# An mLSTM cell before a cosine-gated feed-forward on one Trainium2 core: the state's increment by head in two column halves, one transpose for y's last columns, and another order of the first weight conversions

## The chip, the cores and the metric

The kernel runs on one core of a Trainium2 chip. Its metric is the device time of one execution in microseconds (us). The profile that is read here is of one execution of the same program; its span is 553.4 us.

## The reference, cut to what matters

```python
batch, n_heads, seq, head_dim = (4, 8, 768, 40)          # B, H, S, D
for t in range(S):
    m_new  = np.maximum(f_gate[:, :, t] + m, i_gate[:, :, t])
    f_stab = np.exp(f_gate[:, :, t] + m - m_new)
    i_stab = np.exp(i_gate[:, :, t] - m_new)
    m = m_new
    C = f_stab * C + i_stab * np.einsum('bhd,bhe->bhde', vt, kt)     # state, 40 x 40 for each head
    n = f_stab * n + i_stab * kt
    h_tilde = np.einsum('bhde,bhe->bhd', C, qt)
    denom   = np.maximum(np.abs(np.einsum('bhd,bhd->bh', n, qt)), 1.0)
    y[:, :, t] = sigmoid(o_gate[:, :, t]) * h_tilde / denom
x = y.transpose(0, 2, 1, 3).reshape(3072, 320)
h = x @ w_in                                             # 320 x 2048, float64
out = ((h * np.cos(h)) @ w_out).astype(float32)          # 2048 x 320, float64
```

## The kernel before, in words

The recurrence over 768 steps is computed in chunks of 128 steps. A cell is one chunk of one batch: 6 chunks by 4 batches make 24 cells, numbered n = 4 c + b. A cell computes, for its 8 heads, the scores inside the chunk (`scores`, `ps`), weighs them with the decay (`weigh`), applies them to v (`values`, `ph`), adds what the kept state gives (`values_kept`, `pq`), divides and gates (`normalize`), and makes the increment of the state for the next chunk. Cells 0 to 7 write y with time on the partitions (`z`) and turn it on TensorE (`px`); cells 8 to 23 compute y already turned (`values_turned`, `hp`) and have no `px`. The last chunk, cells 20 to 23, needs no increment.

The state's increment is `pu` = (k weighed)ᵀ · [v, 1]. `weigh_k` (L387) multiplies k, which lies in tiles of 64 elements a head with zeros behind the 40, by a weight of each step on GpSimd, 128x512 elements. `seam` (L580) then takes the heads in pairs: 104 columns of two heads' k are the stationary operand (head one at 0 to 39, head two at 64 to 103), the 82 columns of both heads' v move. Of the four blocks that come out two are wanted, those of a head with itself; they lie at partitions 0 to 39 and 64 to 103. `state` copies them (chunk 0, ScalarE, L594) or adds them (later chunks, VectorE, L596) into the kept state.

The feed-forward works on a chunk of all 4 batches, 512 tokens. `Up(c, f2)` multiplies two blocks of 128 features: the first 256 rows of x by L613, 128 rows a time, the last 64 rows by L616, where two blocks of features share the array by row halves; x's last 64 rows therefore lie twice, at partitions 0 to 63 and 64 to 127. `near` and `sin` (ScalarE), `rest` and `gate` (VectorE) make h cos h, and `down` (L645) accumulates the output. Each cell of chunk c + 1 is interleaved by hand with two `Up` and two `down` of chunk c (`both_parts`), and the order in which Python issues the work is each engine's queue order (`manual_schedule`).

`normalize` writes z in two parts: L537 writes the first 256 columns; L542 the last 64, once in chunk 0, and twice side by side in chunk 1. In chunk 1 one transpose (L571) turns these doubled 128 columns. In chunk 0 two matmuls against the identity (L575) turn the one copy of 64 columns into each half of the partitions.

The weights come as float64 bit patterns. `parts` (two ScalarE passes, L140 and L142) and `join` (three VectorE passes L146, L148, L150, and an integer addition on GpSimd, L151) make float32 of them, a piece at a time. The first `Up` needs the three pieces of w_in's first quarter: two of 512 columns (`w_in_sb`) and one of 256 (`w_in_l`, the operand of L616). The temporaries `wt` and `wm` have two buffers each.

`first_cells` (L659 to L769) orders cells 0 to 3, which nothing of the feed-forward can overlap. Its end is what the change touches:

```python
        weigh(3)
        join(*parts(*pieces.pop(0)))      # w_in, first piece
        ...
        seam_out(2); state(2); gates_keep(*pg)
        values(3); normalize(3)
        turn(B)
        join(*parts(*pieces.pop(0)))      # second piece
        warm(3); seam(3)
        decay_exponents(B); load_E(B + 2)
        seam_out(3)
        join(*parts(*pieces.pop(0)))      # third piece, w_in_l
        state(3)
```

Of the kernel before, what the change touches and what calls it, by code (L numbers as in the profile page):

```python
# [11 lines left out]
FP = mybir.dt.float32  # L12
I32 = mybir.dt.int32
# [3 lines left out]
OP = mybir.AluOpType  # L17
# [12 lines left out]
def kernel(  # L30
# [20 lines left out]
    nc = tc.nc  # L51

    B, H, S, D = q.shape
# [13 lines left out]
    DA, DL, T4 = 32, 8, 4  # L67
    assert DM - NK * 128 == 64 and NF % 4 == 0 and DA + DL == D
    NB = 4
    PR = 64 + D  # L70
    TURNED = 2 * B
    SPREAD = (0, 1)

# [68 lines left out]
        nc.scalar.activation(out=m, in_=lo, func=AF.Copy, scale=2.0 ** -29)  # L142
        return dst, hi, t, m

    def join(dst, hi, t, m):
        nc.vector.tensor_scalar(out=t.bitcast(FP), in0=t.bitcast(FP), scalar1=LEAST, scalar2=GREATEST,  # L146
                                op0=OP.max, op1=OP.min)
        nc.vector.tensor_scalar(out=t, in0=t, scalar1=5, scalar2=2, op0=OP.logical_shift_left,  # L148
                                op1=OP.logical_shift_right)
        nc.vector.scalar_tensor_tensor(out=t, in0=hi, scalar=TOP2, in1=t, op0=OP.bitwise_and, op1=OP.bitwise_or)  # L150
        nc.gpsimd.tensor_tensor(out=dst.bitcast(I32), in0=t, in1=m, op=OP.add)  # L151

    def block(f2, e):

# [203 lines left out]
    def cols(n, j, width):  # L358
        c, b = divmod(n, B)
        return tab[:, c, j, ts(b, H)].unsqueeze(2).to_broadcast([128, H, width])  # L360


    def decay_exponents(n):
        E = Es[n]
        nc.vector.tensor_tensor(out=E, in0=E, in1=cols(n, 0, C), op=OP.subtract)  # L365
        nc.gpsimd.affine_select(out=E, in_=E, compare_op=OP.is_ge, fill=1.0e30, base=0,  # L366
                                pattern=[[0, H], [1, C]], channel_multiplier=-1)
# [15 lines left out]

    def weigh_k(n):
        if n < N - B:
            kw = p2.tile([128, H, 64], FP, name="kw", tag="kw")
            nc.gpsimd.tensor_tensor(out=kw, in0=ks[n % NB], in1=cols(n, 1, 64), op=OP.mult)  # L387
            kws[n] = kw

    def psum(n):  # L390
# [3 lines left out]
    def pair(t, p):  # L394
        return t[:, 2 * p:2 * p + 2].rearrange("p j d -> p (j d)")
# [122 lines left out]
    def normalize(n):  # L518
        c, b = divmod(n, B)
        pq, hs = heads_of[n]  # L520
        if n >= B:
            ph = hs
            hs = p1.tile([128, H, D1], FP, name="hs", tag="hs")
            nc.vector.tensor_tensor(out=hs, in0=pq, in1=cols(n, 2, D1), op=OP.mult)
            nc.vector.tensor_tensor(out=hs, in0=hs, in1=ph, op=OP.add)
        dn = p2.tile([128, H], FP, name="dn", tag="dn")

        nc.vector.scalar_tensor_tensor(out=dn, in0=hs[:, :, D], scalar=-TWO_PI, in1=least, op0=OP.mult, op1=OP.max)
        nc.vector.scalar_tensor_tensor(out=dn, in0=hs[:, :, D], scalar=TWO_PI, in1=dn, op0=OP.mult, op1=OP.max)
        nc.vector.reciprocal(out=dn, in_=dn)  # L530
        y = p1.tile([128, H, D], FP, name="y", tag="y")
        o = sig[c][:, ts(b, DM)].rearrange("t (h d) -> t h d", h=H)
        nc.vector.tensor_tensor(out=y, in0=o, in1=hs[:, :, 0:D], op=OP.mult)

        z = p1.tile([128, DM + 64], FP, name="z", tag="z")
        za = z[:, 0:NK * 128].rearrange("t (i k d) -> t k i d", i=2, k=HP)
        nc.vector.tensor_tensor(out=za, in0=y[:, :, 0:DA].rearrange("t (k i) d -> t k i d", i=2),  # L537
                                in1=dn.rearrange("t (k i) -> t k i", i=2).unsqueeze(3).to_broadcast([128, HP, 2, DA]),
                                op=OP.mult)
        twice = 1 if n < B else 2  # L540
        shape = [128, twice, H, DL]
        nc.vector.tensor_tensor(out=z[:, NK * 128:NK * 128 + 64 * twice].rearrange("t (e h d) -> t e h d", e=twice, h=H),  # L542
                                in0=y[:, :, DA:D].unsqueeze(1).to_broadcast(shape),
                                in1=dn.unsqueeze(1).unsqueeze(3).to_broadcast(shape), op=OP.mult)
        ys[n] = z
# [17 lines left out]
    def seam(n):  # L563

        pool, tag = psum(n)
        if n < TURNED:
            px = pool.tile([128, NK + 1, C], FP, name="px", tag=tag)
            for i in range(NK):
                nc.tensor.transpose(px[:, i], ys[n][:, ts(i, 128)], ident)
            if n >= B:  # L570
                nc.tensor.transpose(px[:, NK], ys[n][:, NK * 128:], ident)  # L571
            else:

                for e in range(2):
                    nc.tensor.matmul(px[64 * e:64 * e + 64, NK], ys[n][:, NK * 128:DM], ident, start=True, stop=True)  # L575
            pxs[n] = px
        if n < N - B:
            pu = pool.tile([128, HP, 2, D1], FP, name="pu", tag=tag)
            for p in range(HP):
                nc.tensor.matmul(pu[0:PR, p].rearrange("p j d -> p (j d)"), pair(kws[n], p)[:, 0:PR],  # L580
                                 vs[n % NB][:, 2 * p:2 * p + 2].rearrange("p j d -> p (j d)"), start=True, stop=True)
            pus[n] = pu

    def seam_out(n):
        c, b = divmod(n, B)
        if b == 0:
            xT[c] = p2.tile([128, NK + 1, B, C], FP, name="xT", tag="xT")
        nc.scalar.copy(out=xT[c][:, :, b], in_=pxs[n])

    def state(n):  # L590
        if n < N - B:
            for j, r, s in halves(n):
                if n < B:
                    nc.scalar.copy(out=s, in_=pus[n][r, :, j])  # L594
                else:
                    nc.vector.tensor_tensor(out=s, in0=s, in1=pus[n][r, :, j], op=OP.add)  # L596


    gs, po = {}, {}
# [59 lines left out]
    def first_cells():  # L659
        nc.vector.memset(nil, 0.0)  # L660
        gates_in()
        nc.scalar.copy(out=ident_b, in_=ident)
        load(0, "qk")
        later_gates_in()
        load(0, "v")
        load(1, "qk")
        load_o(0, (0, 1))
        load(1, "v")
        load(2, "qk")
        load_E(0)  # L670
        load_E(1)
        warm(12)
        wall_in(0, 0, pmu)
        wall_in(0, 1, psum_o())
        gates_first()
        gates_first_out()
        spread(0, 0)
        decay_exponents_half(0, 0)
        turn(0)
        turn_out(0, False)  # L680
        gates_sums()
        spread(0, 1)
        decay_exponents_half(0, 1)
        decay(0)
        weigh_k(0)
        load_E(2)
        load(2, "v")
        load_E(3)
        load_o(0, (2, 3))
        load(3)  # L690
        pieces.extend(weights_in(0))
        wall_in(1, 0, psum_o())
        wall_in(1, 1, psum_o())
        gates_less_sums()
        spread(1, 0)
        decay_exponents_half(1, 0)
        scores(0)
        gates_maxima()
        turn(1)
        weigh(0)  # L700
        sigmoid(0, slice(0, 2))
        turn_out(1, False)
        spread(1, 1)
        decay_exponents_half(1, 1)
        gates_exponents()
        decay(1)
        weigh_k(1)
        values(0)
        normalize(0)
        scores(1)  # L710
        gates_exp()
        turn(2)
        turn_out(2, False)
        warm(2)
        seam(0)
        weigh(1)
        seam_out(0)
        state(0)
        load(B)
        decay_exponents(2)  # L720
        gates_diagonal()
        decay(2)
        weigh_k(2)
        values(1)
        load_E(B)
        load_o(1)
        load_E(B + 1)
        outs.append((0, weights_out(0)))
        normalize(1)
        scores(2)  # L730
        turn(3)
        sigmoid(0, slice(2, 4))
        seam(1)
        weigh(2)
        decay_exponents(3)
        turn_out(3)
        seam_out(1)
        values(2)
        decay(3)
        weigh_k(3)  # L740
        state(1)
        normalize(2)
        scores(3)
        pg = gates_turn()
        warm(1)
        seam(2)
        weigh(3)
        join(*parts(*pieces.pop(0)))
        pieces.extend(weights_in(1))
        load(B + 1)  # L750
        outs.extend((p, weights_out(p)) for p in range(1, 3))
        seam_out(2)
        state(2)
        gates_keep(*pg)
        values(3)
        normalize(3)
        turn(B)
        join(*parts(*pieces.pop(0)))
        warm(3)
        seam(3)  # L760
        decay_exponents(B)
        load_E(B + 2)
        seam_out(3)
        join(*parts(*pieces.pop(0)))
        state(3)
        turn_out(B, False)
        decay(B)
        weigh_k(B)
        sigmoid(1)  # L769
# [161 lines left out]
```

## Time and profile before

The time is 555.97 us, the median of three runs (555.28 to 556.11).

| Engine | busy us | share of the span | instructions |
|---|---|---|---|
| PE (TensorE matmul) | 542.2 | 98% | 3247 |
| PEld (weight load) | 322.9 | 58% | 3247 |
| DVE (VectorE) | 351.0 | 63% | 690 |
| ACT (ScalarE) | 262.8 | 47% | 418 |
| POOL (GpSimd) | 85.8 | 16% | 114 |

TensorE's granted clock is 1.00 in every stretch. A float32 matmul shows as two records, a float32 transpose as one. In the rows of the views, `out<-in` gives the tiles by the program's names, `128*104` the rows and columns of the stationary operand, `128x82` partitions by elements of the moving one, and `xN` how many records the row merges. In brackets stands how long the engine was idle before the row and what ended that; "issue" means that the profile shows nothing it waited for. Records of matmuls overlap[...]: the distance between starts tells what one costs in a stream.

### The profile page before, as it was taken

How to read it: one execution, taken by the hardware profiler on the slowest of the kernel's cores; microseconds unless marked ns; L12 is line 12 of the kernel's file. 1: busy time of each engine (PE TensorE's matmuls, PEld its weight loads, DVE VectorE, ACT ScalarE, POOL GpSimd, SP SyncE). 2: the span in 40 equal slices, each digit the busy share in tenths (PEclk: the TensorE clock that was granted, in tenths of full speed). 3: DMA queues.
4: the chain of work that ended last, by engine and by line, in shares of the span. 5: the costliest groups of instructions: out<-in, count | busy, mean ns of one | idle time of the engine just before them, and what ended most of it. 6: DMA issues, size and time to landing. Idle time of an engine off the chain costs nothing.

```text
span 553.4 us, 8844 instructions
## 1 busy us (share of the span) xinstructions
PE 542.2 (98%) x3247; PEld 322.9 (58%) x3247; DVE 351.0 (63%) x690; ACT 262.8 (47%) x418; POOL 85.8 (16%) x114
## 2 busy tenths in 40 slices
PE   8998999999999999999999999999999999999997
PEld 5865566665665565565555555656655655555554
DVE  5877967757777677577667667666766765322321
ACT  4869686774632544543436345327345332332312
POOL 6542533523110100101101101100000000000000
PEclk9999999999999999999999999999999999999999
DMA  9999969560265751166634065635065000000001
GB/s 141 230 199 251 237 167 226 133 149 3 72 139 119 157 118 45 49 137 141 154 82 89 13 167 129 136 79 121 7 160 120 8 15 12 30 22 1 0 0 47
DMA packets 134507, 56.80 MB, mean 103 GB/s; under 512 B 72080, under 2 KB 130528, under 8 KB 134464
## 3 DMA queue, kind: packets, MB, share of 16 engines
q1 hardware_dynamic: 134320, 56.04, 45.7%
q8 instruction: 25, 0.41, 0.3%
q0 software_dynamic: 96, 0.18, 0.1%
q14 instruction: 18, 0.15, 0.1%
q10 hardware_dynamic: 48, 0.02, 0.0%
HBM read 50.00 MB, written 6.21 MB: 102 GB/s over the span
## 4 chain that ended last, share of the span: by engine, by line
PE 90%; DVE 5%; POOL 2%; issue 1%; ACT 1%; DMA 0%; POOLq 0%; ACTq 0%; DVEq 0%
PE po L645 38%; PE pup L613 29%; PE pup L616 9%; PE ps L440 4%; PE hp L483 3%; PE pu L580 3%; PE ph L465 2%; PE hp L477 2%; DVE wt L146 1%; PE pt L421 1%; DVE wt L150 1%; DVE wt L148 1%; POOL w_out_sb L151 1%; PE pq L455 0%; DVE n L624 0%
## 5 line engine op out<-in xcount | busy, mean ns | idle before, releaser
L645 PE MATMUL po<-w_out_sb,g 128*128 128x320 f32 x768 | 218.5, 438 | 2.7 <-POOL w_out_sb L151 2.7
L645 PEld LDWEIGHTS po<-w_out_sb,g 128*128 128x128 f32 x768 | 142.1, 190 | 68.0 <-issue 8.3
L613 PE MATMUL pup<-xT,w_in_sb 128*128 128x512 f32 x384 | 175.2, 598 | 0.8 <-POOL w_in_sb L151 0.5
L621 ACT ACTIVATE n<-pup 128x512 int32<-128x512 f32 x96 | 52.0, 593 | 218.2 <-PE pup L616 218.2
L624 DVE SCALAR_TENSOR_TENSOR n<-pup,n 128x512 f32<-128x512 f32 x96 | 61.9, 686 | 139.5 <-ACT n L621 139.5
L613 PEld LDWEIGHTS pup<-xT,w_in_sb 128*128 128x128 f32 x384 | 70.8, 190 | 77.5 <-issue 66.5
L366 POOL TENSOR_SCALAR_AFFINE_SELECT E<-E 128x1024 f32<-128x1024 f32 x19 | 20.8, 1094 | 286.9 <-DVE E L365 248.3
L629 ACT ACTIVATE n<-n 128x512 f32<-128x512 f32 x96 | 58.8, 630 | 11.6 <-DVE n L624 11.6
L633 DVE SCALAR_TENSOR_TENSOR g<-pup,n 128x512 f32<-128x512 f32 x96 | 61.7, 685 | 1.7
L616 PE MATMUL pup<-xT,w_in_l 64*128 64x512 f32 x192 | 54.2, 641 | 0.9 <-POOL w_in_l L151 0.9
L616 PEld LDWEIGHTS pup<-xT,w_in_l 64*128 64x128 f32 x192 | 14.4, 184 | 37.4 <-issue 34.9
L374 ACT ACTIVATE E<-E 128x1024 f32<-128x1024 f32 x21 | 22.2, 1058 | 23.1 <-POOL E L366 18.5
L446 DVE TENSOR_TENSOR E<-ps,E 128x512 f32<-128x512 f32 x48 | 30.7, 680 | 3.4 <-PE ps L440 3.4
L405 DVE STREAM_TRANSPOSE t<-qs 128x512 f32<-128x512 f32 x32 | 32.3, 1088 | 0.0
L440 PEld LDWEIGHTS ps<-t,t 40*128 40x128 f32 (+1 forms) x384 | 25.0, 188 | 9.7 <-issue 9.2
L440 PE MATMUL ps<-t,t 40*128 40x128 f32 (+1 forms) x384 | 25.8, 274 | 0.0
L374 ACT ACT_TABLE_LOAD x18 | 23.1, 1283 | 0.3
L776 ACT ACT_TABLE_LOAD x18 | 23.1, 1283 | 0.3
L365 DVE TENSOR_TENSOR E<-E,tab 128x1024 f32<-128x1024 f32 x19 | 23.1, 1215 | 0.0
L497 DVE STREAM_TRANSPOSE room<-hp 128x128 f32<-128x128 f32 x32 | 8.6, 306 | 22.5 <-PE hp L483 22.5
L580 PEld LDWEIGHTS pu<-vs,kw 128*104 128x104 f32 x160 | 16.2, 171 | 9.8 <-issue 9.8
L387 POOL TENSOR_TENSOR kw<-ks,tab 128x512 f32<-128x512 f32 x20 | 20.9, 1043 | 0.1
(130 smaller groups left out, 444.2 us busy)
## 6 DMA issues: line engine op xcount, KB each, us to landing
E<-M_d SPq DMA_DIRECT2D x22, 512.0 KB
bits<-in_moe_w_in_dram SPq DMA_DIRECT2D x40, 128.0 KB
bits<-in_moe_w_out_dram SPq DMA_DIRECT2D x8, 640.0 KB
room<-G_d SPq DMA_DIRECT2D x32, 128.0 KB
ks<-in_k_dram SPq DMA_DIRECT2D x24, 160.0 KB
vs<-in_v_dram SPq DMA_DIRECT2D x24, 160.0 KB
out_dram<-o_sb SPq DMA_DIRECT2D x24, 160.0 KB
qs<-in_q_dram SPq DMA_DIRECT2D x32, 80.0 KB
```

Of the source, the lines that this page charges most:

```text
L374: nc.scalar.activation(out=Es[n], in_=Es[n], func=AF.Exp, scale=-1.0)
L405: nc.vector.transpose(out=dst.rearrange("r p (t x) -> r p x t", x=T4), in_=src.rearrange("r p (x d) -> r p x d", x=T4)[:, :, :, 0:32])
L440: nc.tensor.matmul(ps[j][:, p], kT[r, p], qT[r, p], start=True, stop=True)
L446: nc.vector.tensor_tensor(out=w, in0=pss[n][j], in1=w, op=OP.mult)
L580: nc.tensor.matmul(pu[0:PR, p].rearrange("p j d -> p (j d)"), pair(kws[n], p)[:, 0:PR], vs[n % NB][:, 2 * p:2 * p + 2].rearrange("p j d -> ...
L613: nc.tensor.matmul(pu, w_in_sb[:, i, ts(block(f2, e), 128)], x(i), start=(i == 0), stop=False)
L616: nc.tensor.matmul(pu, w_in_l[r, f2], x(NK, r), start=False, stop=True)
L621: nc.scalar.activation(out=self.n[e], in_=self.pu[e], func=AF.Copy, bias=0.25)
L624: nc.vector.scalar_tensor_tensor(out=self.n[e].bitcast(FP), in0=self.pu[e], scalar=0.25, in1=self.n[e], op0=OP.add, op1=OP.subtract)
L629: nc.scalar.activation(out=r, in_=r, func=AF.Sin, scale=TWO_PI_DOWN)
L633: nc.vector.scalar_tensor_tensor(out=g, in0=self.pu[e], scalar=TWO_PI, in1=self.n[e].bitcast(FP), op0=OP.mult, op1=OP.mult)
L645: nc.tensor.matmul(po[c][b], gs[c, f][:, ts(b, C)], w_out_sb[:, f], start=(f == 0), stop=(f == NF - 1))
```

## The change

Three edits. First, the increment of the state is made head by head: eight matmuls of 40 stationary and 41 moving columns in the place of four of 104 and 82. The even heads' results go to partitions 0 to 39, the odd heads' to 64 to 103 of the same PSUM tile, which is half as large, so the two heads of a pair lie in the two column halves of the array. The block products that were thrown away are not computed, `weigh_k` handles 40 elements a head and not 64, and `state` reads the same partitions as before.

Second, z's last 64 columns are written twice in chunk 0 too, and one transpose makes both halves there, as in chunk 1; the pair of matmuls against the identity is gone.

Third, in `first_cells` the second piece of w_in is joined before `gates_keep`, `values(3)` and `normalize(3)`, the third before `seam_out(3)` and cell 4's `decay_exponents`, and the third piece's integer addition is done by VectorE in the place of GpSimd. In the built program this addition is one instruction of another kind, over 128x512 16-bit halves.

```diff
-    def join(dst, hi, t, m):
+    def join(dst, hi, t, m, last=None):
...
-        nc.gpsimd.tensor_tensor(out=dst.bitcast(I32), in0=t, in1=m, op=OP.add)
+        (last or nc.gpsimd).tensor_tensor(out=dst.bitcast(I32), in0=t, in1=m, op=OP.add)
...
-            kw = p2.tile([128, H, 64], FP, name="kw", tag="kw")
-            nc.gpsimd.tensor_tensor(out=kw, in0=ks[n % NB], in1=cols(n, 1, 64), op=OP.mult)
+            kw = p2.tile([128, H, D], FP, name="kw", tag="kw")
+            nc.gpsimd.tensor_tensor(out=kw, in0=ks[n % NB][:, :, 0:D], in1=cols(n, 1, D), op=OP.mult)
...
-        twice = 1 if n < B else 2
-        shape = [128, twice, H, DL]
+        shape = [128, 2, H, DL]
...
-            for i in range(NK):
+            for i in range(NK + 1):
                 nc.tensor.transpose(px[:, i], ys[n][:, ts(i, 128)], ident)
-            if n >= B:
-                nc.tensor.transpose(px[:, NK], ys[n][:, NK * 128:], ident)
-            else:
-                for e in range(2):
-                    nc.tensor.matmul(px[64 * e:64 * e + 64, NK], ys[n][:, NK * 128:DM], ident, start=True, stop=True)
...
-            pu = pool.tile([128, HP, 2, D1], FP, name="pu", tag=tag)
+            pu = pool.tile([128, HP, D1], FP, name="pu", tag=tag)
             for p in range(HP):
-                nc.tensor.matmul(pu[0:PR, p].rearrange("p j d -> p (j d)"), pair(kws[n], p)[:, 0:PR],
-                                 vs[n % NB][:, 2 * p:2 * p + 2].rearrange("p j d -> p (j d)"), start=True, stop=True)
+                for j in range(2):
+                    nc.tensor.matmul(pu[64 * j:64 * j + D, p], kws[n][:, 2 * p + j], vs[n % NB][:, 2 * p + j],
+                                     start=True, stop=True)
...
         seam_out(2)
+        join(*parts(*pieces.pop(0)))
         state(2)
         gates_keep(*pg)
         values(3)
         normalize(3)
         turn(B)
-        join(*parts(*pieces.pop(0)))
         warm(3)
         seam(3)
+        join(*parts(*pieces.pop(0)), nc.vector)
+        seam_out(3)
         decay_exponents(B)
         load_E(B + 2)
-        seam_out(3)
-        join(*parts(*pieces.pop(0)))
         state(3)
```

More of the change, by code (lines that the diff above doesn't have):

```diff
@@ L69 @@
     NB = 4
-    PR = 64 + D
     TURNED = 2 * B
@@ L539, in normalize @@
                                 op=OP.mult)
-        twice = 1 if n < B else 2
-        shape = [128, twice, H, DL]
-        nc.vector.tensor_tensor(out=z[:, NK * 128:NK * 128 + 64 * twice].rearrange("t (e h d) -> t e h d", e=twice, h=H),
+        shape = [128, 2, H, DL]
+        nc.vector.tensor_tensor(out=z[:, NK * 128:].rearrange("t (e h d) -> t e h d", e=2, h=H),
                                 in0=y[:, :, DA:D].unsqueeze(1).to_broadcast(shape),
@@ L593, in state @@
                 if n < B:
-                    nc.scalar.copy(out=s, in_=pus[n][r, :, j])
+                    nc.scalar.copy(out=s, in_=pus[n][r])
                 else:
-                    nc.vector.tensor_tensor(out=s, in0=s, in1=pus[n][r, :, j], op=OP.add)
+                    nc.vector.tensor_tensor(out=s, in0=s, in1=pus[n][r], op=OP.add)
     gs, po = {}, {}
```

## The prediction

> **What bounds the kernel now.** I read the page's chain of waits first, then its groups, then busy time by stage, then the timeline of one cell of each kind.
>
> ```profile
> PE 90%; DVE 5%; POOL 2%; issue 1%; ACT 1%; DMA 0%; POOLq 0%; ACTq 0%; DVEq 0%
> L580 PEld LDWEIGHTS pu<-vs,kw 128*104 128x104 f32 x160 | 16.2, 171 | 9.8 <-issue 9.8
> ```
>
> TensorE is 90% of the chain. The windows (columns: stretch, length, then busy time of PE, PEld, DVE, ACT, POOL with counts, clock, DMA share, GB/s) say where it is not:
>
> ```profile
> 14.80:34.20 19.40, 19.02 (x188) 16.79 (x189) 14.44 (x33) 16.46 (x29) 9.94 (x12) 1.00 1.05 217
> 34.20:59.40 25.20, 22.68 (x121) 13.68 (x120) 20.65 (x41) 20.84 (x33) 10.53 (x11) 1.00 1.02 234
> 128.00:390.00 262.00, 261.11 (x1744) 152.58 (x1744) 183.55 (x370) 116.12 (x167) 28.68 (x31) 1.00 0.46 103
> ```
>
> From 128 us on TensorE is never free, so its time there comes off the end one for one. In order of time the chain is TensorE from 14.8 to 34.2 us, then DVE, ACT and POOL in turn up to 67.7 us (a w_out conversion), and TensorE again after that, except for one w_out conversion near 128 us.
>
> A cell of the long stage (timeline: start, length, engine, line):
>
> ```profile
> 212.85 1.13 PE L616 MATMUL pup<-xT,w_in_l 64*128 64x512 f32 x4
> 213.91 0.81 PEld L580 LDWEIGHTS pu<-vs,kw 128*104 128x104 f32 x8 [0.76 <-issue]
> 213.91 0.96 PE L580 MATMUL pu<-vs,kw 128*104 128x82 f32 x8
> 214.71 0.47 PE L645 MATMUL po<-w_out_sb,g 128*128 128x320 f32 x1
> ```
>
> Eight records of pu stand between L616 and L645. The single records start every 92 ns, and L645's data begins to stream 0.84 us after pu's first weight load (its second matmul starts at 215.02, less the 0.27 that one takes).
>
> Then a first cell, in the chain (start, length, what), with PEld's rows of the same time:
>
> ```profile
> 19.68 0.44 PE px L569 x2
> 20.12 0.37 PE px L575 x4
> 20.49 0.89 PE pu L580 x8
> 21.38 1.75 PE ph L465 x16
> ...
> 20.05 0.20 PEld L575 LDWEIGHTS px<-ident,z 128*64 128x64 f32 x4 [0.17 <-issue]
> 20.42 0.81 PEld L580 LDWEIGHTS pu<-vs,kw 128*104 128x104 f32 x8 [0.17 <-issue]
> ```
>
> Before L575 and before L580 TensorE stands still, waiting for nothing shown: the array changes its division. L575's two matmuls, in two column halves, start 7 ns apart.
>
> Last, the end of the first cells:
>
> ```profile
> 37.48 2.11 POOL L151 TENSOR_TENSOR w_in_sb<-wt,wm 128x512 int32<-128x512 int32 x1 [3.26 <-ACT wt L140]
> ...
> 38.38 1.36 DVE L146 TENSOR_SCALAR wt<-wt 128x256 f32<-128x256 f32 x1
> 39.77 1.06 DVE L148 TENSOR_SCALAR wt<-wt 128x256 int32<-128x256 int32 x1
> ...
> 42.57 1.13 PE L616 MATMUL pup<-xT,w_in_l 64*128 64x512 f32 x4 [0.94 <-POOL w_in_l L151]
> ```
>
> POOL and DVE block each other here (L146 at 256 columns took 0.29 at 61.3 us), and the first Up waits for both POOL additions.
>
> [...] before a change the next weight load starts 0.20 us after the last 128-column matmul's start, some 0.09 us after its 0.107 of streaming. [...] the steps are 92; between L575's first and second load of 64 columns lie 55. [...] L146 above ended 0.15 us after POOL's addition.
>
> **The change, part by part.**
>
> *pu in cells 8 to 19.* 16 records in the place of 8, in 8 pairs that overlap. One step is the slower of loading 40 columns ([...] 38) and of streaming 41 float32 columns (L613's 512 take 429 ns, so 34). Eight steps are 0.305 us, after 0.04 for the first load. Entering costs what it did, since L616 is already in another division. Leaving is new: 0.09 of drain, then the 0.107 of a 128-column load in the open. From pu's first load to L645's streaming: 0.04 + 0.305 + 0.09 + 0.107 = 0.54 in the place of 0.84, so 0.30 a cell. Nothing else is due there: in these cells pup's buffers are free 0.9 us or more ahead (gates end at 217.9, the next Up starts at 218.8). 12 x 0.30 = 3.6 us. Bounds of a step: 34 ns (streaming) and 55 (the 64-column load), so 0.17 to 0.33 a cell, 2.0 to 4.0 us in all.
>
> *pu in cells 4 to 7.* There px comes first, in whole-array division, so entering adds a drain as well: 0.107 + 0.09 + 0.54 = 0.74 from the last transpose's start, in the place of 0.84. 0.10 in cells 5 and 6; nothing in 4 and 7, where L645 then waits for POOL's w_out addition. 0.2 us.
>
> *First cells.* px: the third transpose costs 0.109; a drain in front of pu was there before. From px's first load to ph's streaming: 0.44 (three transposes from a first load of 0.107) + 0.09 + 0.54 = 1.07, in the place of 1.56 (20.49 + 0.76 less 19.68). 0.5 us a cell, in cells 0, 1 and 2 on the chain: TensorE brings cell 3's ph 1.5 us earlier, by 32.7. L542 at 128 columns costs DVE 0.066 (284 against 218 ns), hidden behind the first two transposes.
>
> *The joins.* In that time DVE takes the second join. POOL's first addition, 1.27 us, then runs beside it and will block one of its passes, so it ends near 34.4 and not 33.2. normalize(3) follows, z is done near 36.3 (35.8 before), xT near 37.2, the first Up starts at 37.3 (37.26). But POOL has nothing more in hand: its second addition runs from 34.5 to 35.8 (it ended at 39.59), and the third join, alone on DVE, is 0.3 + 0.3 + 0.43 and the new addition. That operation is in no row: 512 elements with two SBUF inputs take 0.68 (L408), [...] I take 0.65, bounds 0.35 and 1.0. w_in_l is there at 38.0. So the Up runs through: 8 x 0.43, a drain, L616 at 41.1, not 42.57. Behind the joins DVE has cell 4's decay_exponents (L365), at 37.95, not 37.25; POOL follows at once, at 39.2 for 39.55, ACT's exp, table load, sigmoid and near by 43.9 for 44.27. weigh of cell 4 no longer waits for ps until 44.69, so DVE reaches the first gate at 46.9 for 48.23, and the second Up comes 1.3 us earlier.
>
> *weigh_k.* POOL at 320 elements: 0.65 to 0.72 (1.04 x 320/512, or with the fixed part that 721 and 1272 ns for 256 and 512 columns in L151 suggest). On the chain once: L146 at 59.31 took 0.91 for 0.42, blocked by L387 from 58.89 to 59.94. 0.3 us.
>
> Sum: 3.6 + 0.2 + 1.3 + 0.3 = 5.4, so 550.6 us. `state` and the transfers cost as before.
>
> **The rivals.**
>
> *A, the halves do not overlap:* 16 steps of 38 ns are 0.61, 0.85 with load and drain: nothing gained in cells 8 to 19, 0.2 lost in 5 and 6, 0.2 for 0.5 in the first cells. With the joins about 1.1 us is left: 554.9. Against it, L575's 7 ns, and L483's 32 records in four column tiles within 1.08 us.
>
> *B, the start gives nothing back:* the two additions block DVE longer, the new operation is slow, or normalize(3) behind the second join makes xT late. 3.8 us remain: 552.2. For it: all of the queue there hangs on DVE, and z is later in my own reckoning.
>
> *C, slower, each record bound by its issue:* [...] Against it, L477's 32 records in 0.67 us.
>
> **How the numbers follow.** Main 62%, B 16%, A 12%, C 6%, and 4% for some loss at the start that I don't see[...]. The likeliest is 550.6. The range takes the sizes of the main case's bounds (a short step, a quick addition, and all of TensorE's 1.5 us kept: 548.8) and reaches to A, 554.9. Faster by over 0.2% (1.1 us): main, B, and half of A, 0.85; within: half of A and a little, 0.07; slower: 0.08.
>
> **What would show it.** pu's 16 records in pairs 7 ns apart, pairs about 38 ns apart, L645 streaming 0.54 after the first load; px's three transposes 109 ns apart; kw at 0.65 to 0.72; POOL's first addition beside the second join, a pass of it stretched; L616 of the first Up near 41 with no wait on w_in_l; the second Up near 47.7. I am wrong where pu's records stand 38 ns apart one by one (A)[...], or where the second Up starts near 49 (B).

## The result and the profile after

The median is 551.95 us (550.62 to 553.82, six executions) against 555.30 before: a ratio of 0.9937, with a 95% interval of 0.9915 to 0.9959, so 3.5 us less (2.3 to 4.7). Forecast were 550.6 us and 5.4 us less. The six executions do not agree, and their mean TensorE clocks differ: 550.62 and 550.64 us at a clock of 1.000; 551.80 and 553.82 at 0.997; 552.76 at 0.994; 552.11 at 0.991. Where the clocks of the kernel before are listed, beside the experiments, they are all 0.999 or 1.000. The clock is not the whole of the spread: a mean of 0.997 stands for one stretch of 3.41 us at half clock (experiment 4 has the working), which by itself costs 1.7 us at most, and 553.82 is 3.2 us above the fastest. The rest of that difference is unexplained. The profile below is of the 550.64 one, whose span is 4.4 us below that of before (548.9 against 553.4).

The page's chain of waits and two rows of the groups, after the change:

```profile
PE 85%; DVE 6%; SPq 4%; POOL 1%; DMA 1%; issue 1%; ACT 1%; POOLq 0%; ACTq 0%; DVEq 0%
...
L574 PEld LDWEIGHTS pu<-vs,kw 128*40 128x40 f32 x320 | 7.8, 118 | 10.5 <-issue 9.8 <-PE px L567 0.5
```

TensorE's share of the chain fell from 90 to 85%; pu's loads are twice as many and half as busy in all. The windows, columns as before:

```profile
14.80:34.20 19.40, 18.10 (x205) 15.85 (x205) 16.59 (x36) 17.75 (x32) 9.11 (x12) 1.00 1.01 202
34.20:59.40 25.20, 22.75 (x138) 13.86 (x139) 19.87 (x42) 19.77 (x29) 8.84 (x9) 1.00 0.98 239
67.80:128.00 60.20, 57.70 (x312) 36.46 (x310) 42.55 (x85) 44.90 (x84) 20.88 (x22) 1.00 0.75 165
128.00:390.00 262.00, 261.93 (x1850) 150.38 (x1852) 185.51 (x372) 115.31 (x166) 23.95 (x31) 1.00 0.47 103
```

From 128 us on nothing changed in kind: TensorE is still never free. The third row is the news. The same stretch before:

```profile
67.80:128.00 60.20, 60.20 (x293) 39.01 (x293) 43.26 (x87) 44.83 (x84) 20.63 (x21) 1.00 0.69 159
```

TensorE was busy for all of 60.20 us; now it stands still for 2.5 of them. About half of that is not new: cell 7's wait of 1.1 us for w_out ended at 128.94 us before, mostly past this stretch, and ends at 128.07 now, inside it. The new wait is in cell 5.

A cell of the long stage in the timeline:

```profile
211.09 1.13 PE L610 MATMUL pup<-xT,w_in_l 64*128 64x512 f32 x4
212.15 0.39 PEld L574 LDWEIGHTS pu<-vs,kw 128*40 128x40 f32 x16 [0.76 <-issue]
212.15 0.51 PE L574 MATMUL pu<-vs,kw 128*40 128x41 f32 x16
212.59 0.84 PEld L639 LDWEIGHTS po<-w_out_sb,g 128*128 128x128 f32 x4
```

Sixteen loads take 0.39 us where eight took 0.81. In the single records the two loads of a pair start at 212.150 and 212.157, the pairs follow every 38 ns on average, and L639 streams 0.542 us after the first load, in each of cells 8 to 19 within 2 ns.

A first cell, and then the end of the first cells (timeline):

```profile
19.69 0.55 PE L567 MATMUL px<-ident,z 128*128 128x128 f32 x3 [0.38 <-ACT t L426]
20.25 0.51 PE L574 MATMUL pu<-vs,kw 128*40 128x41 f32 x16
20.69 1.98 PE L464 MATMUL ph<-vs,E 128*128 128x41 f32 x16
...
33.68 0.69 DVE L149 SCALAR_TENSOR_TENSOR wt<-bits,wt 128x512 int32<-128x512 int32 x1
34.52 1.27 POOL L150 TENSOR_TENSOR w_in_sb<-wt,wm 128x512 int32<-128x512 int32 x1 [1.16 <-DVE dn L527]
37.33 3.67 PE L607 MATMUL pup<-xT,w_in_sb 128*128 128x512 f32 x8 [0.23 <-ACT xT L582]
37.41 0.42 DVE L150 CUSTOM_DVE_ANT_0 w_in_l<-wt,wm 128x512 uint16<-128x512 uint16 x1
40.93 1.13 PE L610 MATMUL pup<-xT,w_in_l 64*128 64x512 f32 x4
46.75 1.29 DVE L627 SCALAR_TENSOR_TENSOR g<-pup,n 128x512 f32<-128x512 f32 x2
47.50 2.84 PE L607 MATMUL pup<-xT,w_in_sb 128*128 128x512 f32 x6 [0.49 <-DVE g L627]
```

ph starts 1.00 us after px (1.54 before). The first Up runs through all eight 128-row matmuls and L610 follows without a wait; the second Up starts at 47.50 for 48.96.

Last, cell 5, first before the change and then after it (timeline). L140 before and L139 after are ScalarE's first pass on the next w_in piece, which waits for the piece's transfer:

```profile
69.48 0.68 ACT L140 ACTIVATE wt<-bits 128x512 f32<-128x512 f32 x1 [0.95 <-DMA bits<-in_moe_w_in_dram]
74.55 1.09 POOL L381 TENSOR_SCALAR_AFFINE_SELECT E<-E 128x1024 f32<-128x1024 f32 x1 [1.34 <-ACT E L380]
76.05 0.44 DVE L533 TENSOR_TENSOR y<-o,hs 128x320 f32<-128x320 f32 x1
76.87 0.28 DVE L542 TENSOR_TENSOR z<-y,dn 128x128 f32<-128x128 f32 x1
80.69 4.57 PE L645 MATMUL po<-w_out_sb,g 128*128 128x320 f32 x16
```

```profile
69.95 0.67 ACT L139 ACTIVATE wt<-bits 128x512 f32<-128x512 f32 x1 [3.14 <-DMA bits<-in_moe_w_in_dram]
72.51 2.45 ACT L379 ACTIVATE E<-E,tab 128x128 f32<-128x128 f32 x8
75.03 1.09 POOL L380 TENSOR_SCALAR_AFFINE_SELECT E<-E 128x1024 f32<-128x1024 f32 x1 [1.35 <-ACT E L379]
75.08 1.18 DVE L540 TENSOR_TENSOR z<-y,dn 128x128 f32<-128x128 f32 x1
78.20 1.54 POOL L150 TENSOR_TENSOR w_out_sb<-wt,wm 128x640 int32<-128x640 int32 x1 [2.08 <-DVE wt L149]
79.80 4.57 PE L639 MATMUL po<-w_out_sb,g 128*128 128x320 f32 x16 [1.14 <-POOL w_out_sb L150]
```

Before, the select (it sets the masked half of the next cell's E to zero) was over at 75.64 us, 0.4 us ahead of y and 1.2 ahead of z's last write. After, the piece arrives 0.5 us later and the select with it, while z comes 1.8 us earlier, and the two meet: z's last write takes 1.18 us for 0.28. The w_out join stands behind z on VectorE, and TensorE waits 1.14 us for it.

Where the gain came and went is read best from the starts of the Ups, the same matmuls in each kernel (us; each gain is the start before less the start after, taken before rounding):

| Up | what lies ahead of it | before | after | gain |
|---|---|---|---|---|
| 2nd | first cells and joins | 48.96 | 47.50 | 1.47 |
| 4th | cell 4 (kw) | 74.79 | 73.00 | 1.78 |
| 5th | cell 5 | 85.97 | 85.08 | 0.89 |
| 10th | cells 6, 7 | 144.94 | 144.08 | 0.87 |
| 34th | cells 8 to 19 | 402.05 | 397.62 | 4.43 |
| last | | 536.20 | 531.77 | 4.43 |

So 1.78 were won by the fourth Up, as forecast (1.3 + 0.3, and a little more), half of it was lost in cell 5, and the long stage added 3.56.

### The profile page after: what moved, and what is told of

Same layout as the page of the kernel before. It is cut to its first block, busy times and chain, and to the rows that moved or that the text cites. A ratio compares the mean times of both kernels' runs of the same rounds, so it can differ in the third digit from the quotient of the medians.

```text
span 548.9 us, 9141 instructions
## 1 busy us (share of the span) xinstructions
PE 535.5 (98%) x3395; PEld 315.7 (58%) x3395; DVE 350.9 (64%) x691; ACT 262.7 (48%) x418; POOL 78.0 (14%) x113
## 4 chain that ended last, share of the span: by engine, by line
PE 85%; DVE 6%; SPq 4%; POOL 1%; DMA 1%; issue 1%; ACT 1%; POOLq 0%; ACTq 0%; DVEq 0%
PE po L639 38%; PE pup L607 28%; PE pup L610 9%; PE ps L439 3%; PE hp L482 3%; SPq L321 2%; PE hp L476 2%; POOL w_out_sb L150 1%; DVE wt L149 1%; PE ph L464 1%; PE pu L574 1%; SPq L292 1%; DMA bits<-in_moe_w_in_dram 1%; SPq L130 1%; DVE wt L147 1%
## 5 line engine op out<-in xcount | busy, mean ns | idle before, releaser
L639 PE MATMUL po<-w_out_sb,g 128*128 128x320 f32 x768 | 219.3, 439 | 4.6 <-POOL w_out_sb L150 4.3
L639 PEld LDWEIGHTS po<-w_out_sb,g 128*128 128x128 f32 x768 | 142.0, 190 | 70.5 <-issue 8.3
L607 PE MATMUL pup<-xT,w_in_sb 128*128 128x512 f32 x384 | 174.7, 598 | 0.7 <-DVE g L627 0.5
L607 PEld LDWEIGHTS pup<-xT,w_in_sb 128*128 128x128 f32 x384 | 71.0, 190 | 76.8 <-issue 64.4
L610 PE MATMUL pup<-xT,w_in_l 64*128 64x512 f32 x192 | 54.2, 641 | 0.0
L610 PEld LDWEIGHTS pup<-xT,w_in_l 64*128 64x128 f32 x192 | 14.4, 184 | 36.4 <-issue 35.6
L139 ACT ACTIVATE wt<-bits 128x512 f32<-128x512 f32 (+2 forms) x20 | 13.4, 671 | 9.6 <-POOL w_in_sb L150 6.2
L482 PE MATMUL hp<-E,vs 128*32 128x128 f32 x512 | 17.3, 276 | 0.0
```

The costliest lines, as they stand in the source:

```text
L482: nc.tensor.matmul(hps[n][j][ts(p, 32), half], vs[n % NB][:, h, lo:lo + DA], Es[n][:, h], start=False, stop=True, skip_group_check=True)
L607: nc.tensor.matmul(pu, w_in_sb[:, i, ts(block(f2, e), 128)], x(i), start=(i == 0), stop=False)
L610: nc.tensor.matmul(pu, w_in_l[r, f2], x(NK, r), start=False, stop=True)
L639: nc.tensor.matmul(po[c][b], gs[c, f][:, ts(b, C)], w_out_sb[:, f], start=(f == 0), stop=(f == NF - 1))
```

## The experiments

**Theories.** Two things are to be explained: the 0.9 us lost in cell 5, and the executions at a lower clock. For cell 5, T1: POOL's select on the next cell's E holds VectorE off z. T2: this stretch is set by the transfers (the w_in piece that ScalarE waits 3.14 us for comes no earlier than before), so what TensorE gains at the start is lost there in any case. For the clock, either the shorter seams leave TensorE too little work, or the spread comes from the transfers.

**1. pu alone.** The kernel before with the new pu and state, reading 40 of kw's 64 columns a head:

```diff
-                nc.tensor.matmul(pu[0:PR, p].rearrange("p j d -> p (j d)"), pair(kws[n], p)[:, 0:PR], ...
+                for j in range(2):
+                    nc.tensor.matmul(pu[64 * j:64 * j + D, p], kws[n][:, 2 * p + j, 0:D], vs[n % NB][:, 2 * p + j],
```

> The kernel before with only pu changed (head by head in two column halves, out of a kw that is still 64 columns a head). Main theory: each of cells 8 to 19 gives 0.30 us, 3.6 us together; cells 5 and 6 give at most 0.1 each; in the first cells each seam gives about 0.3 us, so ph(3) ends some 0.9 us earlier, and what of this is left at the end depends on cell 5, where a select on POOL may fall on z's last write on DVE and hold it for up to 1 us. So 3.6 to 4.5 us below before, 0.992 to 0.9935. Rival (the start is bound by transfers, whatever TensorE does): 3.6 us, 0.9935, and the second Up begins as late as before.

Measured: 551.49 us, 0.9924 (0.9911 to 0.9938), all at a clock of 1.0. The second Up is 0.85 us earlier, the fifth 0.08, the last 3.64: 3.56 from cells 8 to 19, and the start's part lost in cell 5. So pu alone is worth as much as the whole change at the median; at full clock the whole change is 0.8 us below it (spans of 548.9 and 549.7 us). The interval takes in both the main theory's range and the rival's 0.9935, so the time doesn't tell them apart. The second Up did begin earlier, against the rival; but of the 0.9 us at the start only 0.08 is left, which is the rival's outcome.

**2. The start alone.** The changed kernel with pu and kw of before (px by three transposes, the new order, VectorE's addition).

> The changed kernel with pu and kw of the kernel before: px by three transposes, and the new order of the joins with VectorE's addition, alone. Main theory: the second Up begins about 1.4 us earlier than before (47.6 for 48.96), since the joins set it; of this 0.4 to 1.4 us is left at the end: cells 8 to 19 give nothing, and in cell 5 the select on POOL takes up to 1 us back. 0.9975 to 0.9993. Rival: TensorE's seams, not the joins, gave the earlier second Up; then it begins 0.9 us or less earlier.

Measured: 554.79 us, 0.9988 (0.9982 to 0.9995), clocks 0.999 to 1.000. The second Up is 1.03 us earlier, between the 1.4 expected and the 0.9 of the rival; the fifth 0.08. What the joins do shows between the first Up and the second: 10.17 us here and in the changed kernel, 11.70 before and 11.66 with pu alone. So the new joins give 1.5 us there, whatever the seams on TensorE take, and cell 5 takes nearly all that is left of it. The transpose of z's last columns, and the third addition's move to VectorE apart from the new order, were not run by themselves.

**3. pu's halves one after the other.**

```diff
-            for p in range(HP):
-                for j in range(2):
+            for j in range(2):
+                for p in range(HP):
```

> The changed kernel with pu's two loops exchanged: the eight heads of the lower column half first, then the eight of the upper. Main theory (a pair costs one step because its two halves stand side by side in the queue): [...] pu takes 0.28 to 0.30 us more in each of cells 8 to 19, 3.4 to 3.6 us in all; about 0 gain is left there. Rival (any two matmuls of different halves overlap, or the rate is set by issue alone): pu takes as long as in the changed kernel, within 0.05 us a cell.

Measured: 553.05 us, 0.9961 (0.9948 to 0.9975). Neither number came out. From pu's first load to L639's streaming it is 0.721 us in each of cells 8 to 19, for 0.542: 0.18 more, between 0.00 and 0.30. The timeline of a cell:

```profile
213.24 0.57 PEld L574 LDWEIGHTS pu<-vs,kw 128*40 128x40 f32 x16 [0.76 <-issue]
213.25 0.69 PE L574 MATMUL pu<-vs,kw 128*40 128x41 f32 x16
213.86 1.64 PEld L639 LDWEIGHTS po<-w_out_sb,g 128*128 128x128 f32 x7
```

In the single records a first series goes alone from 213.244, at 35 to 41 ns a load. At 213.429 a second series begins beside it with its first load, while two loads of the first series are still to come (213.464 and 213.509), and from there on the two run side by side. So the overlap is real. With the halves issued eight and eight the second begins 0.185 us after the first load, when two loads of the first are still due; with the halves in turn it was 0.007 us (212.150 and 212.157 above). A matmul of the other half, too, started (213.431) ahead of three that were issued before it (213.462, 213.507 and 213.545). The records don't name the half; which series is which is read from their spacing, which is nearly the same in both.

**4. kw 64 columns a head again**, of which pu reads 40.

```diff
-            kw = p2.tile([128, H, D], FP, name="kw", tag="kw")
-            nc.gpsimd.tensor_tensor(out=kw, in0=ks[n % NB][:, :, 0:D], in1=cols(n, 1, D), op=OP.mult)
+            kw = p2.tile([128, H, 64], FP, name="kw", tag="kw")
+            nc.gpsimd.tensor_tensor(out=kw, in0=ks[n % NB], in1=cols(n, 1, 64), op=OP.mult)
```

> The changed kernel with kw 64 columns a head again (pu reads 40 of them). Main theory: the fourth Up (73.00 in the changed kernel) begins 0.3 us later, because the 1.05 us product holds the first pass of a join in cell 4 again, 0.3 us at the end or nothing, if cell 5 takes it up. Rival (kw's length is hidden): the same time as the changed kernel and the same start of the fourth Up.

Measured: 552.84 us, 0.9948 (0.9935 to 0.9960), and mean clocks of 0.991, 0.996, 0.991, 0.997 and 0.991. On kw: from the third to the fourth Up the gain over before grows by 0.00 us; in the changed kernel it grew by 0.33. So kw's length is worth 0.33 there; in 1 and 2, which have the 64 columns and the full clock, the gain doesn't grow either, and in 3, which has 40, it grows by 0.33. The more important finding is another, in the windows of its profile (columns as before):

```profile
26.75:30.16 3.41, 2.97 (x36) 2.65 (x35) 3.07 (x9) 3.35 (x6) 2.11 (x2) 1.00 0.93 194
30.16:33.57 3.41, 3.41 (x29) 2.66 (x27) 2.82 (x5) 2.85 (x7) 1.27 (x1) 0.50 0.87 166
33.57:36.98 3.41, 3.41 (x18) 3.41 (x18) 2.40 (x8) 1.45 (x6) 1.27 (x1) 0.50 1.03 200
36.98:40.40 3.42, 3.42 (x26) 2.19 (x25) 2.98 (x7) 0.64 (x2) 0.15 (x1) 0.50 0.92 197
```

The clock is halved for three stretches of 3.41 us, which is 5.1 us of 551 lost in clock and just the mean of 0.991; one stretch gives 0.997, two 0.994, the values that the changed kernel's executions show. In the stretch ahead of 30.16 TensorE was busy for 2.97 of 3.41 us by the records, and its longest stand-still was 0.44 us (the row at 29.83 in this timeline, a wait for `state`'s copy):

```profile
28.52 0.86 PE L265 MATMUL pg<-ident,room 32*128 32x32 f32 x11
29.83 0.54 PE L266 MATMUL pd<-F,one 32*128 32x128 f32 x2 [0.44 <-ACT st L588]
30.30 0.61 PE L651 MATMUL pw<-nil 128*128 128x512 bf16 x1
30.70 0.85 PE L567 MATMUL px<-ident,z 128*128 128x128 f32 x3
```

px's three transposes take 0.85 us here, 0.49 in the changed kernel's profile at full clock. The first Up starts at 40.15 for 37.33, and ph(3) took 3.6 us.

**5. More warm-up work.** Five more matmuls of zeros in the first cells, which compute nothing that is read:

```diff
         turn(3)
+        warm(1)
...
+        warm(1)
         pg = gates_turn()
-        warm(1)
+        warm(2)
...
-        warm(3)
+        warm(6)
         seam(3)
```

> The changed kernel with five more warm-up matmuls of 0.21 us on TensorE in the first cells: one ahead of seam(1), one ahead of gates_turn, two in the place of one ahead of seam(2), six in the place of three ahead of seam(3). Theory (the shorter seams leave TensorE so little work between 23 and 36 us that its clock is halved for one to three stretches of 3.4 us in most executions, which the mean clock of 0.991 to 0.997 and the spread of 550.6 to 553.8 us show): the mean clock is 1.000 in every execution, and all of them lie near the fastest of the changed kernel, 550.5 to 551.0 us; the added work itself costs nothing, since the join holds normalize(3) 1.3 us past ph(3). Rival (the spread comes from the transfers): the clock stays below 1 in most executions or the spread stays, with a median near 552.

Measured: 550.90 us, 0.9926 (0.9914 to 0.9937). Four executions of five at 0.999 or 1.000 (550.73 to 551.09), one at 0.996 (551.72). The first Up comes 0.4 us later than in the changed kernel (37.73), so the added work is not quite free: the four executions at full clock lie 0.1 to 0.4 us above the changed kernel's two. The median is 1 us lower, though the two intervals overlap. With the three early ones alone:

> The changed kernel with only the three early warm-up matmuls (ahead of seam(1), of gates_turn and of seam(2)), without the three ahead of seam(3). Theory (the clock falls for what TensorE does between 23 and 30 us, where the seams got shorter): the mean clock is 0.999 to 1.000 in at least four executions of five, 550.5 to 551.0 us, as with all five. Rival (the stand-still of 0.6 to 1.5 us ahead of px(3), between 33.4 and 36.1 us, does it): a mean clock of 0.991 to 0.997 in most executions and a median of 551.5 to 552.5, as in the changed kernel.

Measured: 551.34 us, 0.9940 (0.9924 to 0.9955), clocks 1.000, 0.999, 1.000, 0.997, 0.994 and 0.994. Three of six are at full clock, between the two expectations: the early ones are not enough. With all five it is four of five here and 11 of 14 in the kernel of 7 and the second and third of 8, whose first cells are the same: 15 of 19 together, for two of six in the changed kernel and none of five in 4. (The second kernel of 6 and the first of 8 also stand still for 2 us in cell 6, and are not counted here.) Kernels 1, 2 and 3, each with some of the shortened parts at their old length, kept 0.999 to 1.000 in all their executions. This fits the theory that more work on TensorE keeps the clock up. It doesn't settle it: no execution of the changed kernel at a lower clock was profiled, so where the clock fell there is not shown, and in its profile at full clock TensorE was busy for only 2.13 us from 33.57 to 36.98 without any fall. What lowers the clock stays open.

**6. exp and select ahead of the w_in piece.** In cells 5 to 7, to get the select out of z's way, once in the kernel before and once in the changed one with the warm-up of 5:

```diff
-        elif pieces:
-            join(*parts(*pieces.pop(0)))
         if begin or more and c > 0:
             decay(n + 1)
         elif more:
             decay_by_bias(n + 1)
+        if pieces and not begin:
+            join(*parts(*pieces.pop(0)))
```

> The kernel before with one order changed: in cells 5 to 7 the eight exp and the select on POOL stand ahead of the conversion of the next w_in piece, which waits for its transfer on ScalarE. Theory[...]: in the kernel before only cell 7 is hit, where y took 1.29 us for 0.44; so 0.85 us less at the end, 554.5, 0.9985, and the wait for w_out near 128 us shrinks from about 1.0 to 0.15 us. Rival (the transfers bound this stretch): the same time as before.

> The changed kernel with the added warm-up matmuls and the same order of exp and select ahead of the piece in cells 5 to 7. Theory: the 0.9 us that z's last write lost in cell 5 and the 0.85 that y lost in cell 7 both come back: 1.7 us below the changed kernel with warm-up alone, near 548.9; the fifth Up begins about 1.8 us earlier than before, as the fourth does. Rival (the transfers take back what TensorE gains at the start, with or without the select): the fifth Up begins 0.9 us earlier than before, as in the changed kernel, and the time is 0.0 to 0.85 below.

Measured: 557.48 us (1.0041, 1.0028 to 1.0054) and 552.68 us (0.9968, 0.9957 to 0.9980): slower than their bases by 2.4 and 1.8 us, so both theories and both rivals missed. In the second, seven of twelve executions were at a clock of 1.000 (552.41 to 552.70), five at 0.997 or 0.994 (554.24 to 555.84): the clock doesn't explain the loss. The timeline of the second one's cell 5:

```profile
71.04 1.09 POOL L380 TENSOR_SCALAR_AFFINE_SELECT E<-E 128x1024 f32<-128x1024 f32 x1 [4.68 <-ACT E L379]
71.56 0.85 DVE L145 TENSOR_SCALAR wt<-wt 128x512 f32<-128x512 f32 x1 [2.62 <-ACT wt L139]
73.52 0.49 DVE L523 TENSOR_TENSOR hs<-pq,tab 128x328 f32<-128x328 f32 x1
76.22 0.28 DVE L540 TENSOR_TENSOR z<-y,dn 128x128 f32<-128x128 f32 x1
80.04 4.57 PE L639 MATMUL po<-w_out_sb,g 128*128 128x320 f32 x16 [0.97 <-POOL w_out_sb L150]
```

z's write is short again, but the piece's join now comes later, at 71.56, and its passes stand in front of hs on VectorE. One obstacle was traded for another. In cell 6 it is worse: by the measure of the table under 8, TensorE waits 2.0 us for the w_out addition (1.9 in the kernel before with this order, 0.2 without it). And in cell 7 the edit did not keep the two apart: the select still fell on y in the kernel before with this order (1.36 us), and on z's first write in the changed one (1.21). The order of two queues had been moved at once, so T1 and T2 are not told apart here.

**7. The select alone moved.** With the warm-up of 5; everything on ScalarE and VectorE keeps its order, and on POOL the select, taken out of `decay_by_bias` as `mask`, goes behind the next w_in addition:

```diff
         if h:
             join(*h)
+        if c == 0 and more and not begin:
+            mask(n + 1)
```

> The changed kernel with the five added warm-up matmuls, and in cells 5 to 7 the select on the next cell's decay alone moved: on POOL it now stands behind the addition of the w_in piece that follows the second Up, and everything on ScalarE and VectorE keeps its order. Theory[...]: z's last write in cell 5 takes 0.28 us again for 1.18, y in cell 7 0.44 for 1.29; w_out is ready that much earlier, the fifth Up begins 1.3 us earlier than before, as the fourth does, and the time is 1.7 us below the version with warm-up alone, 549.2. Rival (the transfers, or another part of the loop from ph to w_out, take it back): the writes are short but the fifth Up begins no earlier, and the time stays at 550.9.

Measured: 549.67 us, 0.9905 (0.9891 to 0.9918). Its cell 5:

```profile
75.44 0.29 DVE L542 TENSOR_TENSOR z<-y,dn 128x128 f32<-128x128 f32 x1
77.67 1.55 POOL L150 TENSOR_TENSOR w_out_sb<-wt,wm 128x640 int32<-128x640 int32 x1 [4.22 <-ACT spot L774]
79.27 4.57 PE L641 MATMUL po<-w_out_sb,g 128*128 128x320 f32 x16 [0.25 <-POOL w_out_sb L150]
```

The fourth Up is 1.42 us earlier than before and the fifth 1.41: nothing is lost in cell 5. In cell 7, where y took 1.36 us on the select in the kernel before and in the changed one, it takes 0.44, and the ninth Up gains another 0.93. Up to the last Up that is 5.84 against 3.99 with warm-up alone: 1.85 us, for 1.75 expected. (Between the medians it is 1.2: this kernel's profile has 0.44 us more after the last Up than the one with warm-up alone, 17.60 for 17.16, and that one's profiled execution lies 0.2 above its median.) T1 stands and T2 falls: the w_in piece came no earlier (69.72 us), and the gain still went through.

The other profiles bear it out. In those of before, of the changed kernel and of 1, 2, 3 and 5 the select starts 5.1 us after ScalarE takes up the w_in piece, whenever that is (69.48 to 70.72 us). What it meets depends on how early VectorE comes: nothing in the kernel before, z's first write in 1 (1.19 us for 0.42), y in 2 and in 5 with all the warm-up (1.37 and 1.36), z's last write in the changed kernel, the first pass of the w_out join in 3 (0.79 for 0.48).

**8. The w_out additions on VectorE.** `join(*h, nc.vector)` in `out_join`, once with the order of 6, once with warm-up alone, once with the select moved:

> The same once more, with the additions of the w_out joins of cells 4 to 7 on VectorE as well. VectorE's new addition took 0.42 us for 256 columns, so 1.04 for 640, in the place of 1.54 and a hand-over of 0.13 on POOL: each wait of TensorE for w_out in these cells (0.9, 0.2, 0.3 and 0.2 us) gets up to 0.6 us shorter, but VectorE has 1 us more to do in each. Theory: 0.5 to 1.2 us below the version without it, 548 us. Rival (VectorE is full there, so the gates come later): no gain, or slower by up to 1 us.

> The changed kernel with the five added warm-up matmuls, and the last addition of the w_out joins of cells 4 to 7 on VectorE (0.83 us for 640 columns in the run before, against 1.54 and a hand-over of 0.13 on POOL). Theory (TensorE waits for this chain in each of these cells): each wait for w_out, 0.9, 1.1, 0.3 and 1.0 us, gets up to 0.75 us shorter, 1.0 to 2.5 us together: 548.4 to 549.9. Rival (VectorE is full there: the gates come later by the 0.83 us): no gain or a loss of up to 2 us.

> Both at once: the select moved and the w_out additions on VectorE, with the warm-up matmuls. Theory: TensorE's waits for w_out in cells 4 to 7, 3.3 us together, are all but gone: 547.6 to 548.2. Rival: another wait, for a gate or for w_in, takes their place, and the time is that of the better of the two single changes.

Measured: 554.73 us (0.9995, 0.9986 to 1.0003), 550.09 us (0.9913, 0.9899 to 0.9927) and 549.32 us (0.9889, 0.9876 to 0.9903).

- The first, with the order of 6, is 2.0 us above the same kernel without the new addition, past both expectations. Twelve of its thirteen executions had a mean clock of 0.997 or 0.994. In its profile the clock was halved from 105.89 to 109.30 us, after a stretch of 3.41 us in which TensorE was busy for 1.54 (the wait in cell 6), so not in the first cells. The one execution at full clock took 553.06 us, still 0.5 above those of 6.
- The second is 0.8 us below 5, short of the 1.0 to 2.5 expected.
- The third is 0.35 us below 7, nearer to the rival's outcome than to the 547.6 to 548.2 expected.

The new addition at 640 columns, in the first of them:

```profile
53.05 0.83 DVE L150 CUSTOM_DVE_ANT_0 w_out_sb<-wt,wm 128x1280 uint16<-128x1280 uint16 x1
53.93 4.58 PE L639 MATMUL po<-w_out_sb,g 128*128 128x320 f32 x16 [0.35 <-DVE w_out_sb L150]
```

It takes 0.83 us for POOL's 1.54. TensorE's wait ahead of po, taken as the time from pu's last matmul to po's streaming less what it is where nothing is waited for (0.13 with the old pu, 0.23 with the new one), in us:

| kernel | cell 4 | cell 5 | cell 6 | cell 7 |
|---|---|---|---|---|
| before | 1.02 | 0.20 | 0.19 | 1.12 |
| changed | 1.16 | 1.22 | 0.33 | 1.25 |
| 5, with warm-up | 1.15 | 1.25 | 0.32 | 1.25 |
| 7, and the select moved | 1.14 | 0.33 | 0.32 | 0.31 |
| 8, w_out addition on VectorE | 0.42 | 0.45 | 0.10 | 1.41 |
| 8, both | 0.42 | 0.29 | 0.00 | 1.01 |

The row "8, w_out addition on VectorE" is the second of the three; its profiled execution had the clock halved from 22.70 to 26.12 us, ahead of these cells. In the second and third kernels the addition helps in cell 4, in cell 5 where the select is not moved, and in cell 6, but not in cell 7. There VectorE meets POOL again: in the second, the first pass of the w_out join took 0.80 us for 0.48 beside the select (from 124.21 us on), and the new addition 1.12 for 0.83 beside POOL's product for kw; in the third, POOL reached the moved select at 121.56 us, for 127.58 in 7, and z's last write took 1.18 once more. With the order of 6, in the first kernel, the wait in cell 5 went from 1.0 to 1.8, and the one in cell 6 stayed at 2.0. The last kernel, 549.32 us, is below both the kernel before and the changed one (551.95).

## Why the prediction was right, and where it was not

*pu in cells 8 to 19, 0.30 a cell, 3.6.* Right: 0.542 us for the 0.54 forecast, 3.56 in all, the same in the changed kernel and with pu alone. The step of 38 ns, which was the author's estimate, and the 7 ns within a pair came out. Rivals A and C fall with it, and 3 shows what A would have cost in part.

*Leaving pu.* Right: the drain and a bare load are in the 0.542. The first load of L639 comes 0.130 us after pu's last matmul starts; 34 of streaming and 90 of drain were forecast. The bare load shows as 0.108 us from L639's first load to its second. Pauses like this drain stand elsewhere in the trace after, from the end of the last matmul's streaming (429 ns for 512 columns) to the next load: 0.091 to 0.092 us between L607 (`128*128`) and L610 (`64*128`), 48 times, and 0.088 to 0.089 between L610 and pu (`128*40`), 12 times; in the trace before, 0.093 to 0.094 between L569 (`128*128`) and L575 (`128*64`), 4 times. Between L639 and L607, both `128*128`, the load comes 0.27 us ahead of that end, 24 times.

*pu in cells 5 and 6, 0.1 each.* Wrong: 0. The table above shows the reason, and it was in the profile of before: po already waited 0.20 and 0.19 us for w_out there. The prediction looked for the wait in cells 4 and 7 alone.

*The first cells.* The seam gave 0.54 for 0.5, and ph(3) ended 1.27 us earlier (32.95 for 34.22) against 1.5. Then nearly every time of the chain came out: the second join at 34.37 (34.4), z at 36.27 (36.3), the first Up at 37.33 (37.3), w_in_l at 37.83 (38.0), L610 at 40.93 (41.1), the first gate at 46.75 (46.9), the second Up at 47.50 (47.7). A pass of the second join was stretched by POOL's addition, as said (L147, 1.38 us). The new addition took 0.42 us, near the low end of the 0.35 to 1.0 that were the author's estimate.

*kw, 0.3.* Right where it arises: 0.72 us, and 0.33 at the fourth Up by 4. What cell 5 then left of it was not measured.

*The sum.* Here it failed: the steps add up to 5.4, the trace has 4.43. The failing step is the reading of the chain behind the first cells, "TensorE again after that, except for one w_out conversion near 128 us": it let every gain at the start count to the end. What the prediction says of the time from 128 us on held (3.56 us of 3.6). In cell 5 the start's gain had to pass through VectorE's y and z, the w_out join behind them and the addition on POOL that po waits for, and there the select, tied to a transfer, had been over only 0.4 us ahead of y. With TensorE 1.8 us earlier it fell on z: 0.9 us back in cell 5, and the two tenths of cells 5 and 6 not there. 7 shows it by taking the cause away. The prediction reckoned with such a hold in the joins, where L146 ended 0.15 us after POOL's addition, and not for the select in cell 5, where z ended 0.14 us after it.

*The clock.* The forecast gave 4% to some loss at the start that it did not see. A lower clock is in four of the six executions, both middle ones among them, so the median lies above the 550.6 of full clock; what lowers it was not shown. That 550.6 is just the time forecast comes of two errors against each other: the base of 555.97 was 0.7 above the median of 555.30, and the sum 0.7 too large against it (4.7 measured at full clock, 4.4 between the two profiles).

Rival B, 552.2, is near the median for another reason than its own: the start did give back 1.5 us at the second Up, and then cell 5 took 0.9 of it, and the executions at a lower clock lost more.

## What to carry to other kernels

Follow a gain past the stage in which it arises: list each later point where the engine that now comes earlier meets work of another engine, with the slack before (0.4 us between the select and y in cell 5 here), and ask what moves with it and what, tied to a transfer, does not. Instructions of VectorE and POOL that missed each other before can meet after: z's last write took 1.18 us beside the select here, for 0.28. And when TensorE's work in a thin stretch is cut, look at its clock over several executions, not in one profile: added matmuls of zeros made the first Up 0.4 us later here, and 15 of 19 executions with them, for two of six without, were at full clock.

## What was not expected of the hardware

- The clock was halved for multiples of 3.41 us after stretches of 3.41 us in which TensorE was busy for 2.97 us (experiment 4; the longest stand-still was 0.44 us) and 3.01 us (the second kernel of 8, ahead of 22.70 us), and once after one in which it was busy for 1.54 us (the first kernel of 8).
- Matmuls of two column halves issued eight and eight, not in turn, still overlap in part: the second series began 0.185 us after the first, and 0.18 us was lost where 0.30 would be lost without any overlap, by the 38 ns a step of the prediction.
- VectorE's integer addition over 16-bit halves took 0.42 us for 256 and 0.83 for 640 int32 columns, a little over half of POOL's 0.72 and 1.54.
